# One transformer block on one core: the first feed-forward matrix computed for pairs of segments with seven block products in place of eight

## The chip, the core and the metric

The program runs on one core of a Trainium2 chip. The core has a matrix engine (TensorE, in the profile PE for its matmuls and PEld for its weight loads), a vector engine (VectorE, DVE), an activation engine (ScalarE, ACT), a general engine (GpSimd, POOL) and a queue engine that issues most transfers (SyncE, SP). Each engine works through its own instructions in order; they meet through semaphores. The metric is the device time in microseconds (us). Three timed runs of the kernel before gave 814.06, 815.38 and 816.48 us; their median, 815.38 us, is the time to compare with.

## What is computed

The input x has 2048 rows of 512 numbers, in four segments of 512 rows. A layer norm with a scale and shift taken from a conditioning vector is followed by attention with 32 heads inside each segment, to which a running memory of the earlier segments is added, and by an output projection; then a second layer norm with scale and shift, a feed-forward net with 1792 hidden units, and a gated sum:

```
h = _layernorm(x) * (1 + ca) + sa
x = x + ga * _A_ref(h, A_wq, A_wk, A_wv, A_wo, A_beta)
h = _layernorm(x) * (1 + cb) + sb
x = x + gb * _B_ref(h, B_w1, B_b1, B_w2, B_b2)

def _B_ref(x, w1, b1, w2, b2):
    h = _gelu(x @ w1 + b1)
    return h @ w2 + b2
```

Every value is float32. The kernel keeps each operand of the large products as a high and a low part (suffixes h and l, type fp32r), and computes a product as three: high by high, low by high, high by low.

## The kernel before

Until about 190 us of the profile it makes the projections for queries, keys and values and the memory of all segments. Then comes attention, a loop over 64 positions P (pairs of heads; two of them make one stack Q, four one group U, sixteen a segment). What each engine does in it is written out in a table of tokens and in positions in tenths of P: `ap(pos, f)` puts a piece of work at pos/10. For each P there are score matmuls for the row maximum (four P ahead, line 609, DVE takes the maximum at line 616), score matmuls for the exponentials (line 698, ACT at lines 713 and 724, POOL masks the diagonal at line 701) and the products with V (line 738). A group U then passes through DRAM: `pv_out` stores to TD, `pv_in` loads it as dn and opk, `den` makes the reciprocal and stores RD, `rb_in` loads it spread over rows as rbB, `mix` multiplies and adds (POOL for U below 13, DVE from 13 on), `o_hi` on ACT and `o_lo` make the two parts oh and ol. With the four groups of a segment s done, `wo_part(s, b, g)` (line 815) makes the output projection for each of its four row blocks b, in the bank mm, and `wo_out` (lines 830 to 834) adds x and stores the block to X2D. For segments 0 to 2 this stands in the attention loop, 12 matmuls to a stack; segment 3 follows the loop.

The second layer norm of segment 0 is in the loop too: `ln2_load`, `ln2_stats`, `ln2_rstd`, `ln2_apply`, and `first_ht`, which turns the segment on PE (line 162, 4 instructions for each of 4 blocks of 128 columns), scales it on ACT (line 170, tile C0h) and splits it into C0hh (DVE) and C0hl (POOL, line 141).

The feed-forward part takes one segment after the other, and in it 14 blocks f of 128 hidden units. `ffn1(n)` makes the 12 matmuls of the first matrix into one of three banks f1b (line 989), the gelu on ACT (line 992, tile gt) and the split into gh and gl on DVE; `ffn2(m)` makes the 12 matmuls of the second matrix into the four banks acc (line 1073). The two alternate, with ffn1 four blocks ahead of ffn2. The first four ffn1 and the whole projection of segment 3 stand between the last product with V and the first ffn2. The weights w1 and w2 are loaded, split and kept during the first segment. `xrt` holds x for the last sum, line 1076, from which the output is stored.

## Time and profile before

| | us |
|---|---|
| three timed runs, median (lowest to highest) | 815.38 (814.06 to 816.48) |
| span of the profiled execution, first to last instruction | 811.6 |
| attention loop | about 190 to 484.6 |
| from the last product with V to the first ffn2 | 484.6 to 509.7 |
| ffn1 and ffn2 alternating, to the end | 509.7 to 811 |

The profiled execution is a run of its own; beside its span the page gives no other time for it. The median lies 3.8 us above the span, and that is taken as what lies around it. A row of an engine's timeline has its start and length in us, the engine, the line, what it writes and reads, and in brackets the engine's idle time before it with what ended it. Matmul rows overlap (each is 0.39 us long for 512 columns); the pace is read from start to start. The DMA table says nothing of landing times here; they are read from the rows that waited for a transfer.

### The profile page before, as it was taken

What the parts mean: (1) busy time and instruction counts of PE and PEld (TensorE: products, weight loads), DVE (VectorE), ACT (ScalarE), POOL (GpSimd) and SP (SyncE); (2) the same over time, 40 slices, a digit from 0 to 9 for tenths busy, and PEclk for the clock granted to TensorE, in tenths of its full rate; (3) what the DMA queues carried; (4) which work ended last, traced back from release to release, by engine and by line L of the source; (5) the groups of instructions that cost most, each with busy time, mean ns of one, the idle gap of its engine ahead of it and who ended that gap; (6) DMA issues with size and microseconds to landing.
All of it is one profiled execution on the core that took longest, in us unless ns stands there. A gap on an engine that the chain in (4) does not pass through costs nothing.

```text
span 811.6 us, 13638 instructions
## 1 busy us (share of the span) xinstructions
PE 796.0 (98%) x4669; PEld 546.9 (67%) x4669; DVE 502.7 (62%) x1373; ACT 368.5 (45%) x734; POOL 287.3 (35%) x508
## 2 busy tenths in 40 slices
...
GB/s 339 183 311 253 271 181 218 159 353 129 171 171 182 165 208 175 238 199 181 177 183 206 172 192 192 213 120 101 25 79 1 52 67 38 1 1 104 1 1 52
DMA packets 83566, 123.03 MB, mean 152 GB/s; under 512 B 14116, under 2 KB 46244, under 8 KB 82984
## 3 DMA queue, kind: packets, MB, share of 16 engines
...
q8 instruction: 36, 0.59, 0.3%
...
## 4 chain that ended last, share of the span: by engine, by line
PE 75%; DMA 8%; ACT 5%; DVE 4%; POOL 4%; issue 3%; SPq 1%; ACTq 0%; DVEq 0%; POOLq 0%
PE acc L1073 18%; PE f1b L989 16%; PE pv L738 6%; PE att L698 5%; PE q L330 5%; PE att L609 5%; PE k L330 4%; PE mm L815 3%; PE v L481 3%; DMA RD<-dn 2%; DMA rbB<-RD 2%; ACT pt L713 1%; PE nu L453 1%; DMA qst<-ms 1%; POOL pt L701 1%
## 5 line engine op out<-in xcount | busy, mean ns | idle before, releaser
L616 DVE CUSTOM_DVE_ANT_0 dump<-att,maskb 128x512 bf16<-128x512 f32 (+2 forms) x384 | 192.2, 553 | 27.2 <-PE att L609 24.3
L992 ACT ACTIVATE gt<-f1b,b1t 128x512 f32<-128x512 f32 x56 | 38.5, 688 | 245.8 <-PE f1b L989 195.0
L713 ACT ACTIVATE pt<-att 128x512 f32<-128x512 f32 (+1 forms) x256 | 126.1, 557 | 44.6 <-PE att L698 44.3
L701 POOL TENSOR_SCALAR_AFFINE_SELECT pt<-pt 128x256 f32<-128x256 f32 x256 | 100.1, 408 | 80.1 <-ACT pt L713 50.1
L140 DVE CAST gh<-gt 128x512 fp32r<-128x512 f32 x56 | 23.8, 425 | 163.0 <-ACT gt L992 163.0
L698 PE MATMUL att<-qst,kst 99*128 99x512 bf16 (+3 forms) x512 | 106.6, 300 | 5.5 <-ACT pt L724 2.1
L609 PE MATMUL att<-kst,qst 96*128 96x512 bf16 (+2 forms) x384 | 94.2, 326 | 0.7 <-DVE nm L616 0.2
L738 PE MATMUL pv<-pt,V 128*32 128x512 f32 (+2 forms) x992 | 88.3, 442 | 0.1
L1073 PE MATMUL acc<-w2h,gh 128*128 128x512 f32 (+1 forms) x224 | 86.7, 387 | 0.0
L1073 PE MATMUL acc<-w2l,gh 128*128 128x512 f32 (+1 forms) x224 | 86.0, 384 | 0.4 <-DVE w2l L141 0.4
L1073 PE MATMUL acc<-w2h,gl 128*128 128x512 f32 (+1 forms) x224 | 85.9, 383 | 0.0
L698 PEld LDWEIGHTS <-kst 99*128 99x128 bf16 x512 | 42.9, 97 | 56.9 <-issue 39.7
L989 PE MATMUL f1b<-hodd,w1h 128*128 128x512 f32 x224 | 73.7, 390 | 0.0
L724 ACT ACTIVATE pt<-att 128x512 f32<-128x512 f32 (+1 forms) x128 | 57.1, 512 | 22.9 <-PE att L609 19.9
L153 POOL TENSOR_SCALAR crs<-cmv 128x4 f32<-128x4 f32 x4 | 1.0, 247 | 170.8 <-DVE cmv L150 170.7
L609 PEld LDWEIGHTS <-qst 96*128 96x128 bf16 x384 | 33.2, 98 | 39.9 <-issue 24.6
L1073 PEld LDWEIGHTS acc<-w2l,gh 128*128 128x128 f32 x224 | 42.0, 188 | 9.1 <-DVE w2l L141 0.9
L989 PEld LDWEIGHTS f1b<-hodd,w1h 128*128 128x128 f32 x224 | 42.1, 188 | 8.6
L1073 PEld LDWEIGHTS acc<-w2h,gl 128*128 128x128 f32 x224 | 42.1, 188 | 8.4
L1073 PEld LDWEIGHTS acc<-w2h,gh 128*128 128x128 f32 x224 | 42.1, 188 | 8.3
L738 PEld LDWEIGHTS pv<-pt,V 128*32 128x32 f32 x992 | 22.2, 108 | 36.8 <-issue 26.2
L989 PE MATMUL f1b<-C0hh,w1l 128*128 128x512 f32 x112 | 43.7, 390 | 0.2 <-DVE w1l L141 0.2
...
## 6 DMA issues: line engine op xcount, KB each, us to landing
...
```

Of the source, the lines that this page charges most:

```text
L330: pe.matmul(ps, a[:, k, 128 * g:128 * g + 128], b[k], start=(k == 0 and i == 0), stop=(k == KB - 1 and i == 2))
L481: pe.matmul(ps, a[k][:, 128 * b:128 * b + 128], w[:, k, :], start=(k == 0 and i == 0), stop=(k == KB - 1 and i == 2))
L609: pe.matmul(ps, q_of(P, h, i), k_of(P, h, 128 * (i + 1)), start=True, stop=True)
L616: v.tensor_tensor_reduce(out=dump[n_dump[0] % 2][:, :n], in0=src, in1=maskb[:, 512 - n:], scale=-1.0, scalar=-4 * NEG, op0=ALU.add, op1=AL ...
L698: pe.matmul(ps, k[:99, e, 128 * j:128 * j + 128], q[:99, e, 128 * j:512], start=True, stop=True)
L701: pool.affine_select(out=t, in_=t, pattern=pattern, compare_op=ALU.is_ge, fill=0.0, base=0, channel_multiplier=-1)
L713: act.activation(pt[:, h, :], ps[:, :n], AF.Exp, scale=0.25)
L724: act.activation(pt, pv_, AF.Exp, scale=0.25)
L738: pe.matmul(ps[32 * c:32 * c + 32, lo:hi], V[4 * s + j][:, VW * hd:VW * hd + 32], pt[:, c % 2, lo - o:hi - o], start=start, stop=stop)
L989: pe.matmul(ps, a[:, k, :], b[k], start=(i == 0), stop=(i == 11))
L992: act.activation(g, ps, AF.Gelu_apprx_tanh, bias=b1t[:, f:f + 1])
L1073: pe.matmul((mm if lo else acc[b])[:, lo:hi], a[:, c], w[:, lo:hi], start=(f == 0 and i == 0), stop=(last and i == 2))
```

## The change

The four segments are handled as pairs, 0 with 1 and then 2 with 3: for a pair all of the first matrix, then all of the second. For the first matrix the columns of a pair are one block matrix with two blocks of 256 input features by two segments, and w1 gives for each j from 0 to 6 two blocks of hidden units (f = j and j + 7) by two of input features. `quad(n)` computes that two by two product with seven block products (`prod`, 6 matmuls each: two blocks of 128 features by three parts) where the code before has eight. For this it needs sums and differences of the operands: `r_sub` forms four differences of segment blocks on DVE, once for a pair, `r_hi` and `r_lo` split seven blocks; `w_sub` forms four sums or differences of weight blocks on POOL for each n, `w_hi` and `w_lo` split six of seven views of them in two buffers that alternate (wt1). The products go to the banks bx, by and bv (two each); three of them are added on while the partial sum is copied out by ACT between products (`s1`, `t2`, `s3`), and DVE adds by or bv to the copies (`add`). `g_out` applies the gelu and stores the block to a new DRAM tensor GD; `load_g` brings it back into a ring of four tiles and `split_g` makes gh (ACT) and gl (DVE) for ffn2, two blocks ahead. The work of quad n on t4 and b22 is done within quad n+1, and after the last quad of a pair in a step with no products of its own.

The output projection of segment 2 leaves the attention loop and stands behind it, in the banks bx0, by0, bv0 and spare; the layer norm of segment 1 enters the loop, and its turning (`ln2_turn`, tiles hr) stands between those blocks. The splitting of segment 0 leaves the loop. The weights of the first matrix are loaded and split again for the second pair. ffn2 takes its banks from both sets in turn and the rows for the last sum go through the tile xt2 of segment 2.

```diff
- 'wo': [[2, 10, 10, 10], [6, 10, 11, 11], [2, 10, 10, 11]],
- 'woout': [10, 11, 11],
...
+ 'wo': [[2, 10, 10, 10], [6, 10, 11, 11]],
+ 'woout': [10, 11],
...
- 'ht': 481,
...
- 'ln': [312, 339, 374, 408],
+ 'ht': [465, 474, 481, 494],
+ 'ln': [[312, 339, 374, 408], [560, 597, 612, 624]],
...
- 'w1at': [58, 59, 60],
+ 'w1at': [58, 60],
...
+    def ln2_turn(s, d, ps=None):
+        ps = ps or mm
+        for b in range(4):
+            pe.transpose(ps[:, 128 * b:128 * b + 128], xt2[s][b][:, 128 * d:128 * d + 128], ident)
+        h = ce.tile([128, 512], F32, tag="hr", bufs=8, name=f"hr{s}_{d}")
+        act.activation(h, ps, AF.Identity, bias=cols[:, 2, d:d + 1], scale=cols[:, 3, d:d + 1])
+        hr[s, d] = h
...
+        def load_w1(j):
+            r = wmp.tile([128, 4, 2, 128], F32, tag="wm", bufs=4, name=f"wa{j}")
+            for i in range(2):
+                f = j % FH + FH * i
+                sp.dma_start(r[:, 2 * i:2 * i + 2].rearrange("p a k n -> p (a k) n"),
+                             w1[:, 128 * f:128 * f + 128].rearrange("(k p) n -> p k n", p=128))
+            wa[j] = r
...
-        for s in range(NSEG):
+        for s in range(NSEG - 1):
...
-        def first_ht(d):
-            h, l = transposed(ce, ce, lambda: mm, xt2[0], 0, 2, "C0", 4, 1, (d,),
-                               lo=pool if PRM["htlo"] == "p" else v)
...
-            ap(PRM["ht"] + PRM["htd"] * d, own, "mm", ("h", d), first_ht, (d,), True)
...
+            ap(PRM["ht"][d], own, "mm", ("h", d), ln2_turn, (0, d), True)
...
+        spare = pf.tile([128, 512], F32, name="spare")
+        bx, by, bv = [[pf.tile([128, 512], F32, name=f"{n}{i}") for i in range(2)] for n in ("bx", "by", "bv")]
...
+        def r_sub(p, n):
+            x, y = {"t1": ("b12", "b11"), "t2": ("b22", "b11"), "t3": ("b22", "b12"), "t4": ("b21", "b22")}[n]
+            for o, i, j in zip(hk(p, RAW[n]), hk(p, x), hk(p, y)):
+                v.tensor_tensor(out=o, in0=i, in1=j, op=ALU.subtract)
...
+        def r_hi(p, n):
+            for k in range(2):
+                act.activation(R[n][0][k], hk(p, RAW.get(n, n))[k], AF.Copy)
...
+        def w_sub(j, i):
+            if i == 0:
+                wb[j] = wmp.tile([128, 4, 2, 128], F32, tag="wm", bufs=4, name=f"wb{j}")
+            a, b = wa[j], wb[j]
+            x, y = ((a[:, 2], a[:, 3]), (b[:, 0], a[:, 0]), (a[:, 0], a[:, 2]), (a[:, 1], b[:, 1]))[i]
+            pool.tensor_tensor(out=b[:, i], in0=x, in1=y, op=ALU.add if i == 0 else ALU.subtract)
...
+        def prod(n, name, ps, start):
+            t, i = PW[name]
+            wh, wl = wt1[t][n % 2]
+            rh, rl = R[name]
+            for k in range(2):
+                for c, (a, b) in enumerate(((wh, rh), (wl, rh), (wh, rl))):
+                    pe.matmul(ps, a[:, i, k, :], b[k], start=start and k == 0 and c == 0, stop=k == 1 and c == 2,
+                              skip_group_check=not start)
+        def g_out(n, src, dst, half, seg):
+            f = n % FH + FH * half
+            act.activation(dst, src, AF.Gelu_apprx_tanh, bias=b1t[:, f:f + 1])
+            sp.dma_start(GD[2 * (n // FH) + seg][f], dst)
+        def add(t, ps):
+            v.tensor_tensor(out=t, in0=ps, in1=t, op=ALU.add)
...
+        def quad(n, first, last):
...
+            X, Y, V_, t2 = bx[n % 2], by[n % 2], bv[n % 2], s2[n % 2]
+            X_, V__, t2_ = bx[(n - 1) % 2], bv[(n - 1) % 2], s2[(n - 1) % 2]
+            if not last:
+                prod(n, "b11", X, True)
+                act.activation(s1, X, AF.Copy)
+            if not first:
+                add(s3, V__)
+                g_out(n - 1, s3, s3, 1, 1)
+            step(0)
+            if not last:
+                prod(n, "b21", Y, True)
+                add(s1, Y)
+            step(1)
+            if not first:
+                prod(n - 1, "t4", X_, False)
+            if not last:
+                g_out(n, s1, s1, 0, 0)
+            if not first:
+                g_out(n - 1, X_, s4, 1, 0)
+            step(2)
+            if not last:
+                prod(n, "t2", X, False)
+                act.activation(t2, X, AF.Copy)
+            step(3)
+            if not first:
+                prod(n - 1, "b22", V__, False)
+                add(t2_, V__)
+            step(4)
+            if not last:
+                prod(n, "t1", V_, True)
+            if not first:
+                g_out(n - 1, t2_, t2_, 0, 1)
+            step(5)
+            if not last:
+                prod(n, "t3", X, False)
+                act.activation(s3, X, AF.Copy)
+            step(6)
...
+        for b, ps in enumerate((bx[0], by[0], bv[0], spare)):
+            wops[2, b] = ps
+        for b, ps in enumerate((bx[1], by[1], bv[1], mm)):
+            wops[3, b] = ps
+        rest(15, "pv_in")
...
+        r_hi(0, "b11")
...
+        wo_seg(2, 0, range(4))
+        ln2_turn(1, 0)
...
+        rest(14, "mem_mix", "mix", "o_hi")
+        rest(15, "den", "rb_in")
+        rest(15, "am_in")
...
+        wo_seg(2, 3, range(4))
+        ln2_turn(1, 3)
+        for b in range(4):
+            wo_seg(3, b, range(2))
...
+        for b in range(4):
+            wo_part(3, b, 2)
+        r_lo(0, "t2")
+        rest(15, "mix", "o_hi")
+        r_lo(0, "t1")
+        rest(15, "o_lo")
+        assert not left, left
+        def close_wo():
+            for b in range(4):
...
+        for n in range(2 * FH):
+            j = n % FH
+            if j + 2 < FH:
+                bg(n, 1, load_w1, n + 2)
+                for i in range(4):
+                    bg(n, 5 + i // 2, w_sub, n + 2, i)
+            if j + 1 < FH:
+                for i in range(7):
+                    bg(n, i, w_prep, n + 1, i)
+        bg(0, 1, r_hi, 0, "t3")
+        bg(0, 2, r_lo, 0, "t3")
+        bg(0, 1, ln2_load, 2)
+        bg(0, 3, close_wo)
+        bg(0, 4, r_sub, 0, "t4")
+        bg(0, 5, r_hi, 0, "t4")
+        bg(0, 6, r_lo, 0, "t4")
...
+        for s, n in ((2, 1), (3, 3)):
+            for b in range(4):
+                bg(n, 1 + b, ln2_stats, s, b)
+            bg(n, 5, ln2_rstd, s)
+            for i in range(2):
+                bg(n, 8 + i, ln2_applies, s, 2 * i, 2 * i + 2)
+            for d in range(KB):
+                bg(n, 10 + d, ln2_turn, s, d, (mm, spare)[d % 2])
...
+        ring = [[s1, s2[1 - p], s3, s4] for p in range(2)]
+        def load_g(p, m):
+            sp.dma_start(ring[p][m % 4], GD[2 * p + m // FB][m % FB])
+        def split_g(p, m):
+            h, l = gx[0](f"gh{p}{m}"), gx[0](f"gl{p}{m}")
+            ghs.append((h, l))
+            split(h, l, ring[p][m % 4], v, act)
+        for p in range(2):
+            n = FH * p + FH
+            bg(n - 1, 5, load_g, p, 0)
+            bg(TAIL + n, 5, load_g, p, 1)
+            bg(TAIL + n, 5, load_g, p, 2)
+            bg(TAIL + n, 5, load_g, p, 3)
+            bg(TAIL + n, 6, split_g, p, 0)
+            bg(TAIL + n, 6, split_g, p, 1)
...
+        for i in range(2):
+            fbg(1, i, load_w1, FH + i)
+        for i in range(4):
+            fbg(1, 3, w_sub, FH, i)
+            fbg(1, 12, w_sub, FH + 1, i)
+            fbg(1, 10 + i, w_hi, FH, i)
+            fbg(1, 10 + i, w_lo, FH, i)
...
+        accs = [bx[1], by[1], bv[1], mm], [bx[0], by[0], bv[0], spare]
...
-        for n in range(AHEAD, NSEG * FB + AHEAD):
...
-            if n < NSEG * FB:
-                if n > AHEAD:
-                    ffn1(n)
...
-                ffn2(m)
+        NM = 2 * FB
+        for p in range(2):
+            for j in range(FH + 1):
+                quad(FH * p + j, j == 0, j == FH)
+            xres = xt2[2]
+            for m in range(NM):
+                s, f = 2 * p + m // FB, m % FB
+                if m + 4 < NM:
+                    load_g(p, m + 4)
+                if m + 2 < NM:
+                    split_g(p, m + 2)
...
+                if p == 0 or m < NM - 3:
+                    ffn2(s, f, ghs.pop(0))
         for b in range(4):
-            for m in range(NSEG * FB - AHEAD, NSEG * FB):
-                ffn2(m, (b,))
+            for i, g in enumerate(ghs):
+                ffn2(NSEG - 1, FB - 3 + i, g, (b,))
+        assert not bgs and not fs
```

What the change makes of the engines' orders, at the places that matter for what follows. First PE, at the end of attention; att3 is the bank of the last products with V, pt the exponentials. Before, the first matrix of segment 0 follows at once:

```order
L738 MATMUL att3_2009<-pt63_3_5902,V15_154 32x128 x2
L738 MATMUL att3_2009<-pt62_2_5857,V14_153 32x256 x2
L738 MATMUL att3_2009<-pt63_2_5897,V14_153 32x256 x2
L989 MATMUL f1b0_5946<-C0hh0_0_4974,w1h0_5987 128x512
L989 MATMUL f1b0_5946<-C0hh0_0_4974,w1l0_5988 128x512
L989 MATMUL f1b0_5946<-C0hl0_0_4975,w1h0_5987 128x512
```

With the change the output projection of segment 2 stands there (bx0 from its first group, U = 8):

```order
L737 MATMUL att3_2065<-pt63_3_5898,V15_210 32x128 x2
L737 MATMUL att3_2065<-pt62_2_5851,V14_209 32x256 x2
L737 MATMUL att3_2065<-pt63_2_5893,V14_209 32x256 x2
L814 MATMUL bx0_5943<-woh_2052,oh8_4713 128x512
L814 MATMUL bx0_5943<-woh_2052,ol8_4715 128x512
L814 MATMUL bx0_5943<-wol_2053,oh8_4713 128x512
```

The 48 matmuls of that projection moved from the loop to this place, and the four ffn1 that stood here are gone from it. Next DVE, before the projection of segment 3 is closed. Before (opk15 is the last group's mix, w1l weights, gl a gelu part):

```order
L140 CAST w1h5_5997<-w1r4_5725 128x512
L141 TENSOR_TENSOR w1l5_5998<-w1r4_5725,w1h5_5997 128x512
L787 TENSOR_TENSOR opk15_6007<-opk15_6007,rbB15_6043 128x512
L789 TENSOR_TENSOR opk15_6007<-opk15_6007,amB15_6009 128x512
L804 TENSOR_TENSOR ol15_6128<-opk15_6007,oh15_6126 128x512
L140 CAST gh3_5964<-gt1_5972 128x512
L141 TENSOR_TENSOR gl3_5969<-gt1_5972,gh3_5964 128x512
L1010 TENSOR_TENSOR w2r0_6144<-w2r0_6144,gab_69 128x512 x2
```

With the change (rt1, rt2, rt3 are splits of the segment differences, hr the turned segments, s10 the first partial sum):

```order
L831 TENSOR_TENSOR xb2_3_5657<-spare_5942,xb2_3_5657 128x512
L997 TENSOR_TENSOR rt2l0_5959<-hr1_2_6081,rt2h0_5957 128x512
L997 TENSOR_TENSOR rt2l1_5960<-hr1_3_6105,rt2h1_5958 128x512
L786 TENSOR_TENSOR opk15_5992<-opk15_5992,rbB15_6055 128x512
L788 TENSOR_TENSOR opk15_5992<-opk15_5992,amB15_6057 128x512
L997 TENSOR_TENSOR rt1l0_5963<-hr0_0_4931,rt1h0_5961 128x512
L997 TENSOR_TENSOR rt1l1_5964<-hr0_1_5008,rt1h1_5962 128x512
L803 TENSOR_TENSOR ol15_6183<-opk15_5992,oh15_6179 128x512
L1041 TENSOR_TENSOR s10_5985<-by0_5945,s10_5985 128x512
L1022 TENSOR_TENSOR w1ml1_5980<-wa1_5736,w1mh1_5979 128x512
L997 TENSOR_TENSOR rt3l0_5967<-hr1_0_6022,rt3h0_5965 128x512
L997 TENSOR_TENSOR rt3l1_5968<-hr1_1_6045,rt3h1_5966 128x512
```

The mix of the last group moved behind the splits and differences of the segment blocks, and the first partial sum follows it. Third PE, in the feed-forward part. Before, ffn2 (acc) and ffn1 (f1b) alternate:

```order
L1073 MATMUL acc3_5952<-w2h7_6191,gh1_5962 128x512
L1073 MATMUL acc3_5952<-w2h7_6191,gl1_5967 128x512
L1073 MATMUL acc3_5952<-w2l7_6192,gh1_5962 128x512
L989 MATMUL f1b2_5948<-hodd00_5953,w1h12_5975 128x512
L989 MATMUL f1b2_5948<-hodd00_5953,w1l12_5976 128x512
L989 MATMUL f1b2_5948<-hodd10_5957,w1h12_5975 128x512
```

With the change, at the end of a pair's first matrix (rt4 and rb22 are the last two products' operands, then ffn2 of block 0):

```order
L1032 MATMUL bx0_5943<-rt4l0_5971,w1th0_5981 128x512
L1032 MATMUL bx0_5943<-rt4h1_5970,w1th0_5981 128x512
L1032 MATMUL bx0_5943<-rt4h1_5970,w1tl0_5982 128x512
L1032 MATMUL bx0_5943<-rt4l1_5972,w1th0_5981 128x512
L1032 MATMUL bv0_5947<-rb22h0_5973,w1th0_5981 128x512
L1032 MATMUL bv0_5947<-rb22h0_5973,w1tl0_5982 128x512
L1032 MATMUL bv0_5947<-rb22l0_5975,w1th0_5981 128x512
L1032 MATMUL bv0_5947<-rb22h1_5974,w1th0_5981 128x512
L1032 MATMUL bv0_5947<-rb22h1_5974,w1tl0_5982 128x512
L1032 MATMUL bv0_5947<-rb22l1_5976,w1th0_5981 128x512
L1309 MATMUL bx1_5944<-w2h0_6244,gh00_6847 128x512
L1309 MATMUL bx1_5944<-w2h0_6244,gl00_6848 128x512
```

No product of another block stands between the last products of the first matrix and the first of the second any more. At that place ACT has (s30, s10, s20, s21, s40 are tiles of the ring, a gelu has b1t among its inputs):

```order
L1037 ACTIVATE s21_5987<-s21_5987,b1t_70 128x512
L1091 ACTIVATE s30_5988<-bx0_5943 128x512
L1037 ACTIVATE s30_5988<-s30_5988,b1t_70 128x512
L1037 ACTIVATE s40_5989<-bx0_5943,b1t_70 128x512
L1037 ACTIVATE s20_5986<-s20_5986,b1t_70 128x512
L134 ACTIVATE gh00_6847<-s10_5985 128x512
L134 ACTIVATE gh01_6851<-s21_5987 128x512
L134 ACTIVATE gh02_6856<-s30_5988 128x512
```

and SP has, with GD0 and GD1 the stored blocks of the two segments:

```order
L1038 DMA GD1_5_144<-s21_5987 128x512
L1249 DMA s10_5985<-GD0_0_125 128x512
L1038 DMA GD1_13_152<-s30_5988 128x512
L1038 DMA GD0_13_138<-s40_5989 128x512
L1038 DMA GD1_6_145<-s20_5986 128x512
L1249 DMA s21_5987<-GD0_1_126 128x512
L1249 DMA s30_5988<-GD0_2_127 128x512
L1249 DMA s40_5989<-GD0_3_128 128x512
```

The split of block 0 stands on ACT behind the last gelu of the first matrix, and the loads of blocks 1 to 3 on SP behind the store of that gelu's block.

391 lines of the change are left out of this document (199 added, 192 removed).

## The prediction

> **What bounds the kernel now.** I read the page's first part, then a table of stretches (start and end; of PE, PEld, DVE, ACT and POOL the busy us and count; granted clock, DMA share, GB/s), then the chain of waits in the feed-forward part.
>
> ```profile
> PE 796.0 (98%) x4669; PEld 546.9 (67%) x4669; DVE 502.7 (62%) x1373; ACT 368.5 (45%) x734; POOL 287.3 (35%) x508
> ...
> 460.00:484.60 24.60, 22.75 (x192) 10.88 (x184) 9.45 (x25) 17.13 (x39) 14.53 (x29) 1.00 0.63 176
> 484.60:509.70 25.10, 24.94 (x110) 20.29 (x110) 18.10 (x31) 6.83 (x10) 2.87 (x2) 1.00 0.62 201
> 509.70:811.00 301.30, 298.14 (x1375) 247.70 (x1373) 128.73 (x240) 50.08 (x76) 4.37 (x6) 1.00 0.17 55
> ...
> 526.90 2.72 PE acc L1073 x12
> 529.62 2.72 PE f1b L989 x12
> ```
>
> PE sets the end. From the last product with V (484.6) on it hardly pauses, the clock is 1.00, and DVE, ACT and POOL are at 43%, 17% and 1% after 509.7. Twelve matmuls of 512 columns take 2.72 us whichever matrix they belong to, so one costs 2.72 / 12 = 0.227 us. A matmul less is time gained, if nothing stops PE in its place.
>
> **What is removed.** The first matrix takes 56 blocks of 12 matmuls, 672; with the change 14 quads of 7 products of 6, 588. 84 x 0.227 = **-19.0 us**. The second matrix, the output projection and the 64 transposes stay in number.
>
> **The projection of segment 2 moves out of attention.** Rows of ACT, one per stack (ms is copied once for each):
>
> ```profile
> 411.58 0.27 ACT L132 ACTIVATE ms<-mm 48x128 bf16<-48x128 f32 x1
> 419.55 0.27 ACT L132 ACTIVATE ms<-mm 48x128 bf16<-48x128 f32 x1
> 429.72 0.27 ACT L132 ACTIVATE ms<-mm 48x128 bf16<-48x128 f32 x1
> 438.11 0.27 ACT L132 ACTIVATE ms<-mm 48x128 bf16<-48x128 f32 x1
> 448.53 0.27 ACT L132 ACTIVATE ms<-mm 48x128 bf16<-48x128 f32 x1
> 458.95 0.27 ACT L132 ACTIVATE ms<-mm 48x128 bf16<-48x128 f32 x1
> 468.57 0.26 ACT L132 ACTIVATE ms<-mm 48x128 bf16<-48x128 f32 x1
> ```
>
> A stack without the projection takes 7.97 us (419.55 less 411.58), the three with 12 matmuls of it take 10.42, 10.42 and 9.62: without them 6.5 us less. The last 12 of the 48 stand after 468.57, where the end hangs on something else:
>
> ```profile
> 465.15 3.07 SPq L839 DMA_DIRECT2D w1r<-in_w  x2
> 469.92 0.38 SPq L776 DMA_DIRECT2D RD<-dn  x1
> 478.20 0.69 DVE L787 TENSOR_TENSOR opk<-opk,rbB 128x512 f32<-128x512 f32 x1 [10.66 <-DMA rbB<-RD]
> 479.72 0.63 ACT L132 ACTIVATE oh<-opk 128x512 fp32r<-128x512 f32 x1 [1.70 <-DVE opk L789]
> 482.26 2.35 PE L738 MATMUL att<-pt,V 128*32 128x512 f32 x28 [1.84 <-POOL pt L701]
> ```
>
> RD of group 13 leaves late, since SP is held by a weight load; so rbB, the mix, oh on ACT, the exponentials behind it and the last products with V are late. With the change two w1 loads stand there for three and no store of X2D before RD, so RD can leave up to 2.2 us sooner. I take 1.5 for this piece, between 0 and the 2.7 of its matmuls. One stack, 419.55 to 429.72, is 2.2 us too long without any projection:
>
> ```profile
> 420.38 1.29 POOL L787 TENSOR_TENSOR opk<-opk,rbB 128x512 f32<-128x512 f32 x1 [2.15 <-DMA rbB<-RD]
> 422.96 1.27 POOL L141 TENSOR_TENSOR C0hl<-C0h,C0hh 128x512 fp32r<-128x512 f32 x1
> 426.74 2.18 PE L738 MATMUL pv<-pt,V 128*32 128x512 f32 x8
> ```
>
> POOL waits for rbB and then has the queue of its masks ahead of PE, with C0hl among it. The change takes the four C0hl off POOL: 1.5 us gained (0 to 2.2). But the same wait can come up in stacks 29 to 31, which become as short: 1.0 lost (0 to 2.2). Attention gives 6.5 + 1.5 + 1.5 - 1.0 = 8.5 us, and behind it the 48 matmuls cost 48 x 0.227 = 10.9: **+2.4 us** (0 to +5).
>
> **The stretch behind attention.** Counted from the last product with V, PE has 84 projection matmuls (19.1) and 16 transposes (four take 0.44, quoted below, so 1.8): 20.9 us of cover, then b11 and b21 (2.7). DVE has, up to the mix of group 15, some 21 instructions of 512 columns at 0.69 and some 3 us of others, 17.5 us, and waits inside for ACT, whose weight split waits for POOL's four w_sub and for group 14's products: I make it 22 to 23 us until that mix. Before, the mix began 15.9 us after the last product:
>
> ```profile
> 496.52 0.59 SPq L782 DMA_DIRECT2D rbB<-RD  x1
> 500.55 0.69 DVE L787 TENSOR_TENSOR opk<-opk,rbB 128x512 f32<-128x512 f32 x1 [0.24 <-DMA rbB<-RD]
> 537.79 0.44 PE mm L162 x4
> ```
>
> Mix (two of 0.69), oh (0.63) and the copy of s1, which stands behind oh on ACT, end at about 25.5; PE wants to overwrite that bank with t2 at 23.6 + 0.8, where 0.8 is a wait I expect at the second turning (mm is read by ACT behind the weight split). So 0.8 + 1.15 there and 0.2 at the first t4, whose operand is at the end of DVE's queue: **+2.2 us** (0, if ACT and DVE run ahead, to +7, if the blocking below strikes each DVE instruction beside POOL's).
>
> **From the first to the second matrix, twice.** Behind the last t3 PE's order has t4, b22 and ffn2 without anything between. Rows:
>
> ```profile
> L992 ACT ACTIVATE gt<-f1b,b1t 128x512 f32<-128x512 f32 x56 | 38.5, 688 | 245.8 <-PE f1b L989 195.0 <-issue 43.6 <-DVE opk L789 7.1
> L138 ACT ACTIVATE w2h<-w2r 128x512 fp32r<-128x512 f32 x14 | 8.8, 626 | 3.1 <-DVE w2r L1010 2.9
> L132 ACT ACTIVATE ts<-att 128x512 f32<-128x512 f32 x1 | 0.6, 597 | 1.8 <-PE att L738 1.8
> ...
> L141 DVE TENSOR_TENSOR gl<-gt,gh 128x512 fp32r<-128x512 f32 x56 | 39.7, 710 | 2.0
> L833 DVE TENSOR_TENSOR xb<-acc,xb 128x512 f32<-128x512 f32 x4 | 2.5, 680 | 0.0
> ...
> 509.42 0.39 PE L989 MATMUL f1b<-C0hl,w1h 128*128 128x512 f32 x1
> ...
> 509.91 0.69 ACT L992 ACTIVATE gt<-f1b,b1t 128x512 f32<-128x512 f32 x1 [2.35 <-PE f1b L989]
> ```
>
> From the end of a matmul's slot (509.42 + 0.23) to ACT's start is 0.26. First, t4 adds onto the bank that ACT still copies to s3: 0.26 + 0.60 + 0.04 = 0.9. Second, behind b22 come an addition on DVE, its gelu, the split of block 0 and only then ffn2's second matmul: 0.26 + 0.68 + 0.69 + 0.63 + 0.71 = 2.97, less the first matmul's slot, 2.75. Third, the load of block 1 is queued on SP behind the store of that last gelu. It issues 1.63 + 0.34 after b22 and takes 4.0, as rbB took (496.52 to 500.55); gh and gl add 1.34, so block 1 is whole at 7.3, where PE, after block 0 and its 2.72, would be at 5.5: 1.6 after the slot of a first matmul. Together 5.25, twice **+10.5 us**. Only the third piece is open: with the 5.84 below it is 3.4, and 0 if it lands as fast as RD of group 15, which was issued at 495.04 and let rbB go at 496.52; both entries then take 7.3 to 14.2.
>
> ```profile
> 459.25 5.84 DMA opk<-TD
> ...
> 495.04 0.32 SPq L776 DMA_DIRECT2D RD<-dn  x1
> ```
>
> The Trainium skill ("SBUF — State Buffer", The DMA setup-cost knee) fits a transfer as about 2 us and its bytes at 436 GB/s, an estimate of 2.6 us for 256 KB; the row of rbB says 4.0 here. By the Trainium skill both entries would cost 2.8 us less.
>
> **Covered work.** In a quad of 42 matmuls, 9.5 us, ACT has three copies (1.8), four gelus (2.75) and 1792 columns of weight splits (about 2.2), 6.8 us; DVE three additions and the low parts, 4.5; POOL four w_sub. A partial copy is due 2.7 us after its product and takes 0.9, so 1.8 us are to spare. GD's stores and loads, 256 KB per 2.4 us, are about 110 GB/s where the table of stretches shows 55 now and 176 at the end of attention. Free while this holds; the rival below has the price. The last three blocks wait about 0.3 once for a buffer: **+0.3 us**.
>
> **The sum.** -19.0 + 2.4 + 2.2 + 10.5 + 0.3 = -3.6 us, against a span of 811.6: 808.0. The median of the runs lies 3.8 above the span, so 815.4 - 3.6 = **811.8 us**.
>
> **Rivals.** One: the waits at the seams are covered. Attention returns all 10.9 us (the projection was its only load there), the stretch behind stalls 0, the loads land within 2 us: -19.0 + 0 + 0 + 7.3 + 0.3 = -11.4, 804 us. For it speaks that DVE stood idle 10.66 us at 478.20; against it that the chain through rbB does not shorten with PE's work. Chance 0.2.
>
> Two: DVE is late behind attention. DVE and POOL hinder each other:
>
> ```profile
> 494.90 1.59 POOL L794 TENSOR_TENSOR amB<-amB,rm 128x512 f32<-128x512 f32 x1 [7.47 <-DMA rm<-rdd]
> 495.38 1.67 DVE L141 TENSOR_TENSOR gl<-gt,gh 128x512 fp32r<-128x512 f32 x1
> ```
>
> An instruction of 0.71 took 1.67 while POOL multiplied. POOL has some 7.8 us there (two multiplications of 1.28, eight halves of that); if each delays DVE by a bit over half its length, 4.5 us more: +0.9, 816.3 us. Against it: most falls in DVE's own waits. Chance 0.17.
>
> Three, on the other side: **the quads are bound by the copies.** PE may not add a product to bx before ACT has copied the partial sum, and ACT, in order, may sit at a gelu whose addition waits on DVE. If the four w_sub of a quad (2.6 us) each stop DVE for their whole length, the additions and low parts slip by 2.6, past the 1.8 to spare: 0.8 us in each of 14 quads, 11 us, -3.6 + 11 = +7.6, 823 us. It decides from a delay of 1.8 us per quad on. For it speaks the row of 1.67; against it that DVE idles half of each quad. Chance 0.16. The Trainium skill ("SBUF — State Buffer", SBUF: two separate sides) says that a two-input DVE instruction and a GpSimd one that reads SBUF exclude each other for whole instructions; the row of 1.67 agrees with it, and by that rule this rival is the likelier.
>
> That the change removes fewer products than it says is ruled out by its order: 588 rows of line 1032.
>
> **Numbers.** My forecast has 0.47, the rivals 0.2, 0.17 and 0.16. What a measurement of this kernel can tell from no change is about 0.3%, 2.4 us: faster is below 812.9, slower above 817.8. Of the forecast's 0.47 some 0.32 lie below 812.9 (the third piece and attention decide), 0.10 between, 0.05 above; of rival two 0.03, 0.11, 0.03. Faster 0.32 + 0.2 + 0.03 = 0.55, same 0.21, slower 0.05 + 0.03 + 0.16 = 0.24. The forecast's own range is 806 to 817. For 8 in 10 the range takes in rival one at its middle, rival two and the lower edge of rival three: 804 to 820.
>
> **What would show it.** 84 matmuls fewer, still 2.72 per 12; the last product with V at 476 (475 to 480) in place of 484.6; PE idle between t3 and the first blocks of ffn2 near 5 us at both places, its end set by gl on DVE and by a load on ACT; no PE idle inside quads; at t2 of quad 0 a wait for ACT of about 1 us. Wrong it would be if the quads take more than 9.6 us, or the entries under 3 us, or if attention ends no sooner.

## The result and the profile after

The changed kernel is slower. Its median is 821.43 us (six runs, 818.84 to 826.18) beside 816.45 us for the kernel before on the same chip; the ratio is 1.0076 (95% interval 1.0050 to 1.0102). The forecast was 811.8 us, with 804 to 820 as the range. The profiled execution has a span of 818.8 us, 7.2 more than the one before. By the medians the difference is 5.0 us: this execution took 820.48 us, 1.7 more than its span, so the profiled execution of the kernel before, with the same 1.7, would have taken 813.3, less than each of its timed runs on this chip. The 3.8 us that the prediction put around the span were 1.7 here.

Each time below is given as a ratio to the kernel before, whose runs were taken between those of the experiment on the same chip. The experiments ran on five chips, so kernels of different chips are compared by these ratios alone. A waiting time or a length of the loop is that of one profiled execution.

The first part of the page after, and two rows of PE's timeline one quad apart (start and length in us, engine, line, operation):

```profile
PE 788.6 (96%) x4585; PEld 535.2 (65%) x4585; DVE 555.7 (68%) x1405; ACT 467.8 (57%) x914; POOL 333.9 (41%) x558
...
521.03 0.39 PE L1032 MATMUL by<-rb21h,w1mh 128*128 128x512 f32 x1
...
530.55 0.39 PE L1032 MATMUL by<-rb21h,w1mh 128*128 128x512 f32 x1
```

PE is down from 98% to 96% of a longer span: it has 84 matmuls fewer in the trace as well (4669 to 4585), and waits more. A full quad takes 530.55 - 521.03 = 9.52 us, 42 matmuls at 0.227, so nothing stops PE inside this quad. Most of the time is lost at three places, which this table of stretches shows (columns as in the prediction):

```profile
450.00:460.00 10.00, 7.64 (x40) 2.72 (x36) 4.20 (x15) 4.12 (x10) 2.39 (x7) 0.66 0.64 190
500.00:510.00 10.00, 8.15 (x36) 6.40 (x35) 9.89 (x14) 2.03 (x6) 5.77 (x5) 1.00 0.55 183
510.00:520.00 10.00, 8.86 (x32) 7.22 (x33) 9.05 (x13) 6.48 (x11) 3.60 (x4) 0.83 0.88 296
560.00:580.00 20.00, 20.00 (x94) 16.55 (x93) 12.23 (x19) 14.73 (x26) 2.38 (x3) 1.00 0.54 181
580.00:595.00 15.00, 11.99 (x44) 8.81 (x43) 6.17 (x10) 6.74 (x11) 0.00 (x0) 0.89 0.78 259
```

The first row lies in the last stacks of attention, the next two behind it, the last at the entry to the second matrix; between them, from 560 to 580, PE is busy all of 20 us. The waits themselves, in PE's timeline (qst holds the queries of a stack, which come from QD, and the row maxima, which are copied into it from ms; pt are the exponentials, s the copies of partial sums):

```profile
453.52 1.04 PE L608 MATMUL att<-kst,qst 96*128 96x512 bf16 x2 [2.36 <-DMA qst<-QD]
...
480.76 2.35 PE L737 MATMUL att<-pt,V 128*32 128x512 f32 x28 [0.75 <-POOL pt L700]
...
511.14 0.78 PE L1032 MATMUL bx<-rt2h,w1mh 128*128 128x512 f32 x1 [3.00 <-ACT s L1060]
...
583.04 0.50 PE L1032 MATMUL bx<-rt4h,w1th 128*128 128x512 f32 x1 [0.74 <-ACT s L1091]
...
588.13 0.51 PE L1309 MATMUL bx<-w2h,gh 128*128 128x512 f32 x1 [2.06 <-ACT gh L134]
```

The second row is the last group of products with V: it ends at 480.76 + 2.35 = 483.1, where the kernel before was at 484.6. The loop has given 1.5 us, not 8.5.

A ledger of the two profiled executions. PE's plain work behind the last product with V is the matmuls at 0.227 and the turnings at 0.44 (four instructions each). Before, that is 1392 and 12, 320.8 us of the 327.0 that it took, a loss of 6.2. Only 0.6 of it lies ahead of the first ffn2, where 108 matmuls and no turning stand in 25.1 us: 48 of the projection of segment 3 and 60 of the first matrix, which are five of its blocks and not four. After, it is 1356 and 12, 312.6 us of 335.7, a loss of 23.1. Up to the end of t3 of quad 6, at 582.15, the changed kernel has 378 and 12, 91.0 us, in 99.1, a loss of 8.1: 1.3 up to the end of b21 of quad 0, 3.2 ahead of t2 of quad 0, 1.7 in a slow pace behind it, and 1.9 later, most of it around the turnings of segments 2 and 3. From the end of t3, 36 matmuls (t4, b22 and two blocks, 8.16 us) took 13.7 and 13.3 us at the two entries.

| term | predicted | measured |
|---|---|---|
| 84 matmuls | -19.0 | -19.0 |
| projection of segment 2, behind the loop | +10.9 | +10.9 |
| the loop without it | -8.5 | -1.5 |
| stretch behind the loop | +2.2 | +7.5 (8.1 less 0.6) |
| two entries | +10.5 | +10.7 |
| the rest | +0.3 | -1.3 |
| sum | -3.6 | +7.3 (spans: +7.2) |

### The profile page after: what moved, and what is told of

Same layout as the page of the kernel before. It is cut to its first block, busy times and chain, and to the rows that moved or that the text cites. A ratio compares the mean times of both kernels' runs of the same rounds, so it can differ in the third digit from the quotient of the medians.

```text
span 818.8 us, 14152 instructions
## 1 busy us (share of the span) xinstructions
PE 788.6 (96%) x4585; PEld 535.2 (65%) x4585; DVE 555.7 (68%) x1405; ACT 467.8 (57%) x914; POOL 333.9 (41%) x558
## 4 chain that ended last, share of the span: by engine, by line
PE 75%; DVE 7%; ACT 6%; DMA 6%; issue 3%; POOL 3%; ACTq 0%; SPq 0%; DVEq 0%; POOLq 0%
PE bx L1032 8%; PE pv L737 7%; PE att L697 6%; PE att L608 6%; PE bx L1309 5%; PE q L314 5%; PE by L1309 5%; PE bv L1309 5%; PE bv L1032 4%; PE k L314 4%; PE v L465 3%; PE spare L1309 2%; PE mm L814 2%; PE mm L1309 2%; PE by L1032 2%
## 5 line engine op out<-in xcount | busy, mean ns | idle before, releaser
L700 POOL TENSOR_SCALAR_AFFINE_SELECT pt<-pt 128x256 f32<-128x256 f32 x256 | 101.4, 413 | 82.8 <-ACT pt L712 49.0
L1007 POOL TENSOR_TENSOR wb<-wa 128x256 f32<-128x256 f32 x28 | 26.9, 962 | 155.5 <-DMA wa<-in_w 147.4
L137 DVE TENSOR_TENSOR gl<-s,gh 128x512 fp32r<-128x512 f32 x56 | 39.9, 712 | 69.5 <-ACT gh L134 69.4
L134 ACT ACTIVATE gh<-s 128x512 fp32r<-128x512 f32 x56 | 35.1, 630 | 83.2 <-PE spare L1309 38.9
L1041 DVE TENSOR_TENSOR s<-bv,s 128x512 f32<-128x512 f32 x28 | 19.3, 688 | 37.7 <-PE bv L1032 29.2
L619 DVE TENSOR_REDUCE nm<-att 128x2 f32<-128x256 f32 x64 | 27.2, 426 | 23.5 <-PE att L655 19.2
L1037 ACT ACTIVATE s<-s,b1t 128x512 f32<-128x512 f32 x42 | 30.3, 721 | 16.2 <-DVE s L1041 16.1
L615 DVE DVE_READ_ACCUMULATOR2_ANT nm<- 128x1 f32 x384 | 31.9, 83 | 0.0
L1309 PE MATMUL bx<-w2h,gh 128*128 128x512 f32 (+1 forms) x70 | 26.4, 377 | 4.1 <-ACT gh L134 4.1
L501 POOL TENSOR_SCALAR qp<-qp 128x512 f32<-128x512 f32 x12 | 18.8, 1564 | 23.1 <-ACT qp L496 23.1
L1309 PE MATMUL bx<-w2h,gl 128*128 128x512 f32 (+1 forms) x70 | 26.4, 377 | 0.2 <-DVE gl L137 0.2
L314 PE MATMUL q<-Ahl,wqh 128*128 128x512 f32 x64 | 25.9, 404 | 0.5 <-DVE Ahl L137 0.5
```

Of the source, the lines that this page charges most:

```text
L134: act.activation(hi, src, AF.Copy)
L137: lo_eng.tensor_tensor(out=lo, in0=src, in1=hi.bitcast(F32), op=ALU.subtract)
L314: pe.matmul(ps, a[:, k, 128 * g:128 * g + 128], b[k], start=(k == 0 and i == 0), stop=(k == KB - 1 and i == 2))
L615: v.tensor_tensor_reduce(out=dump[n_dump[0] % 2][:, :n], in0=src, in1=maskb[:, 512 - n:], scale=-1.0, scalar=-4 * NEG, op0=ALU.add, op1=AL ...
L700: pool.affine_select(out=t, in_=t, pattern=pattern, compare_op=ALU.is_ge, fill=0.0, base=0, channel_multiplier=-1)
L1309: pe.matmul(ps, a[:, c], w[:, lo:hi], start=(f == 0 and i == 0), stop=(last and i == 2))
```

## Experiments

**The three stalls taken one at a time.** First the load that enters the loop.

```diff
- 'ln': [[312, 339, 374, 408], [560, 597, 612, 624]],
+ 'ln': [[312, 339, 374, 408], [574, 602, 615, 624]],
```

> Only the 1 MB load of segment 1 (xt from X2D) is issued later, behind the stack's RD, xb and rbB rows on SP in place of right behind the last kst and qst; its statistics follow 5 places later. Theory: this load shares the DMA engines with the last stack's qst, which took 9.12 us from issue to its first reader, and PE's idle 2.36 us then cost a further 2 us at a granted clock of 0.66. Then the interval between ms rows there falls from 13.09 to 8 to 9 us, the granted clock from 450 to 460 is 1.00, and the time falls by 3.5 to 5 us from 821.4, to about 817. Rival: qst is late through its own chain (ms on ACT, the store to QD); then the interval stays near 13 us and the time near 821. In between, if the wait only goes on to RD and rbB of group 13: the interval falls, the next one grows from 9.50 by as much, and the time stays within 1 us.

Ratio 1.0075 (1.0046 to 1.0104): no gain. The interval of 13.09 fell to 7.72, but its neighbours show where the wait went:

```profile
447.74 0.77 PE L697 MATMUL att<-qst,kst 99*128 99x512 bf16 x3 [1.51 <-DMA qst<-ms]
464.54 0.77 PE L697 MATMUL att<-qst,kst 99*128 99x512 bf16 x3 [1.66 <-DMA qst<-ms]
474.20 1.04 PE L697 MATMUL att<-qst,kst 99*128 99x512 bf16 x2 [3.48 <-DMA qst<-ms]
```

It is no longer qst that is late but the 12 KB of row maxima that go from ms into it, and they are late in three stacks. From the tenth last ms row (the texts ahead of the runs call it that of stack 24) to the end of the last product with V it is 102.0 us; this is called the loop's length below, and it is 102.4 before and 100.4 after. So the load is not the cause by itself.

Then the clock, with matmuls in the gaps at the entries.

```diff
+            if last:
+                fill(n, 3)      # ahead of t4
...
+            if last:
+                fill(n, 9)      # behind b22
```

> Twelve matmuls whose result nothing reads are added at each entry to the second matrix: 3 ahead of t4 of the last quad, 9 behind b22, into a bank that is free. They are 0.7 and 2.0 us of work where PE idles 0.74 and 2.06 us. Theory: the idle time lets the granted clock fall for one stretch of 3.4 us behind each entry (8 matmuls at 0.43 us in place of 0.227), so with PE busy the stretch runs at 0.227 and each entry costs 1.6 us less: 821.4 - 3.2 = 818.2, and the granted clock of 589 to 593 and 736 to 740 is 1.00. Rival: the slow matmuls there wait on operands, not on the clock; then nothing is gained, and the time is 821 to 822.

Ratio 1.0057 (1.0028 to 1.0086): no gain that can be told from the change alone. The granted clock is 1.00 at both entries, but they still lose 4.55 and 4.69 us, the added matmuls counted as lost, against 5.53 and 5.15 in the change. In e1_load_late one entry had no slow stretch without any added matmul, and lost 4.56. So the clock is about 1 us of an entry, and the rest is waiting for data.

Then the order of the entry.

```diff
+                bg(n - 1, m, load_raw, p, m)        # m = 0, 1
+                bg(n - 1, 5 + m, split_g, p, m)
+            bg(n - 1, 6, load_g, p, 2)
+            bg(TAIL + n, 0, ahead, p, 0)            # ffn2 of block 0, ahead of t4
+            bg(TAIL + n, 0, load_g, p, 3)
+            bg(TAIL + n, 4, split_g, p, 2)
+            bg(TAIL + n, 4, ahead, p, 1)            # ffn2 of block 1, behind b22
```

> Blocks 0 and 1 of the second matrix, whose operands were written to GD six quads earlier, are loaded in the quad before the last and split there, and their 24 matmuls stand ahead of t4 and behind b22 of the last quad; blocks 2 and 3 load into the two tiles that the stretch has free first. Theory: an entry costs its 5.3 us because PE's order has only work there that hangs on the last copies and gelus. With 5.44 us of other work between, the copy of s3 (0.9), the addition, gelu and split (2.75) and the next load are all covered: PE idle at both entries falls from 2.8 us each to under 0.5, the clock stays 1.00, and the time falls by 9 to 10.6, to 811 to 812.5. Rival: the loads and splits put into the last full quad collide there with the weights of the second matrix on ACT and DVE and its loads on SP; then the quad grows by 2 us or more and the gain is 5 us or less, 816 or more.

Ratio 0.9965 (0.9938 to 0.9991), 8 to 9 us under the change and a little faster than before. The same stretches of this kernel:

```profile
580.00:590.00 10.00, 10.00 (x45) 8.07 (x44) 4.86 (x8) 5.80 (x10) 0.00 (x0) 1.00 0.84 285
590.00:600.00 10.00, 10.00 (x45) 8.26 (x44) 7.26 (x12) 5.70 (x10) 0.00 (x0) 1.00 0.83 292
```

PE does not pause; the loss at the two entries is 0.18 and 0.14 us. The 10.7 us were a matter of order, with the two tiles more that the new order needs, and the first matrix's gain shows once they are gone.

Last the POOL instructions behind the loop.

```diff
-        for i in range(4):
-            w_sub(1, i)          # behind wo_x(3, 3)
...
+        for j in range(2):       # behind pv_in of group 15
+            for i in range(4):
+                w_sub(j, i)
```

> The four w_sub of quad 1 are taken from behind the last amB on POOL to right behind the four of quad 0, into POOL's idle time from 489 to 502. Theory: behind attention DVE is late because POOL's two-input instructions hold it up: beside w_sub and amB from 502.2 to 508, four r_sub took 3.59 us for 2.5, two w_lo 0.96 each for 0.41, and two r_lo 1.82 for 1.29, 2.7 us in all, and the mix of group 15 hangs on it, then oh and the copy of s1 on ACT, then t2 on PE (3.00 us idle, and 1.6 us more at a low granted clock). With POOL free there the mix comes 2 us or more sooner, t2's wait falls under 1 us, and the time falls by 3 to 4.5, to 817 to 818.5. Rival: DVE's own queue and ACT decide; the instructions that POOL now meets earlier are lengthened in its place, DVE had no slack there, and the time stays within 1 us of 821.4.

Ratio 1.0043 (1.0016 to 1.0070), by the ratios 2.7 us under the change where 3 to 4.5 were expected. The two intervals overlap, so the time alone does not show the gain; the rows do show the mechanism. DVE's rows after, beside POOL's of the same microseconds:

```profile
500.84 3.59 DVE L989 TENSOR_TENSOR hr<-hr,hr 128x512 f32<-128x512 f32 x4
504.36 0.96 DVE L1022 TENSOR_TENSOR w1tl<-wa,w1th 128x256 fp32r<-128x256 f32 x1
...
503.85 1.18 POOL L1007 TENSOR_TENSOR wb<-wa 128x256 f32<-128x256 f32 x1
```

and in this kernel, where POOL is idle there, with two rows from later on:

```profile
500.80 2.49 DVE L989 TENSOR_TENSOR hr<-hr,hr 128x512 f32<-128x512 f32 x4
503.21 0.42 DVE L1022 TENSOR_TENSOR w1tl<-wa,w1th 128x256 fp32r<-128x256 f32 x1
...
523.53 0.60 ACT L1060 ACTIVATE s<-bx 128x512 f32<-128x512 f32 x1 [5.57 <-DMA GD<-s]
524.18 0.69 PE L1032 MATMUL bx<-rt2h,w1mh 128*128 128x512 f32 x1 [3.65 <-ACT s L1060]
```

The rows are short again, the mix of group 15 comes 22.5 us after the last product with V instead of 25.4, and t2 of quad 0 waits 1.23 us instead of 3.00. Then a new wait shows, 3.65 us in quad 1: the copy of s1 stands until the store of s1 to GD has left. I put that to the 1 MB load of segment 2, ahead of the store in SP's queue; the next kernel has it in pieces, among other edits, so this cause was not tested by itself.

**The stalls together.**

```diff
+            if n == 0:
+                rest(15, "o_hi")                    # now behind the copy of s1
+                r_lo(0, "t1")
+                rest(15, "o_lo")
...
-        bg(0, 1, ln2_load, 2)
+        for b, (n, i) in enumerate(((0, 4), (0, 6), (1, 1), (1, 3))):
+            bg(n, i, ln2_piece, 2, b)
```

> The entry order of e3_entry and the early w_sub of e4_wsub_early together, with two more edits: in quad 0 ACT copies s1 before oh of group 15 instead of behind it, and the loads of segments 2 and 3 (1 MB each from X2D) go out as eight pieces of 256 KB over quads 0 to 2, with the statistics of segment 2 one quad later. Theory: what is left of the stall behind attention is ACT's order (in e4_wsub_early the copy of s1 stood 0.5 us behind oh, which waited for the mix; t2 waited 1.23 us) and a store of s1 late behind the 1 MB load (the copy of s1 of quad 1 waited 4.88 us for it and t2 of quad 1 3.65 us). Then both waits go under 1 us and the time is 4 to 6 us under the 813.3 of e3_entry: 807 to 809. Rival: DVE's queue is what is late; then close_wo, which needs oh and ol of group 15, waits in place of t2, 1.5 to 2.5 us, and the time is 810.5 to 812.

Ratio 0.9953 (0.9932 to 0.9974), 1 us under e3_entry by these ratios, which the intervals do not tell apart, so closer to the rival. Both waits at t2 are gone; in their place stand 1.21 us for hr in the turnings, 1.00 for rt4l and 0.92 for a block that DVE normalises.

**The step on the loop.** The projection of segment 2 goes back where it was.

```diff
- 'wo': [[2, 10, 10, 10], [6, 10, 11, 11]],
+ 'wo': [[2, 10, 10, 10], [6, 10, 11, 11], [2, 10, 10, 11]],
...
-        wo_seg(2, 0, range(4))
-        ln2_turn(1, 0)
+        ln2_turn(1, 0, bx[0])
```

> One part of the change is undone: the projection of segment 2 stands in the attention loop again, in the places that it had before, and the four turnings of segment 1 behind the loop use four banks. By the prediction's step the loop gave 6.5 to 8.5 us for taking it out, so with it the length from the ms row of stack 24 to the last product with V goes from 100.5 to 103.8 (the four profiles with this loop so far) to 107 to 112. Theory now: the three stacks are set by chains through DMA (qst, and ms into qst), and the projection ran in their waits; then the length stays at 101 to 104.5. Behind the loop PE has 10.9 us less work, but the mix of group 15 still comes 23 to 26 us after the last product with V, so that part is turned into idle time ahead of t2: I expect 2 to 6 us less in all by the theory, 816 to 820, and by the prediction's step no gain or a loss, 821 to 825.

Ratio 1.0049 (1.0024 to 1.0075). ACT's ms rows of the last stacks, this kernel:

```profile
440.05 0.27 ACT L128 ACTIVATE ms<-mm 48x128 bf16<-48x128 f32 x1
450.47 0.27 ACT L128 ACTIVATE ms<-mm 48x128 bf16<-48x128 f32 x1
460.89 0.27 ACT L128 ACTIVATE ms<-mm 48x128 bf16<-48x128 f32 x1
470.52 0.26 ACT L128 ACTIVATE ms<-mm 48x128 bf16<-48x128 f32 x1
```

and the change:

```profile
438.75 0.27 ACT L128 ACTIVATE ms<-mm 48x128 bf16<-48x128 f32 x1
446.68 0.27 ACT L128 ACTIVATE ms<-mm 48x128 bf16<-48x128 f32 x1
459.77 0.27 ACT L128 ACTIVATE ms<-mm 48x128 bf16<-48x128 f32 x1 [0.47 <-PE mm L676]
469.27 0.27 ACT L128 ACTIVATE ms<-mm 48x128 bf16<-48x128 f32 x1 [0.83 <-PE mm L676]
```

With 36 matmuls more in them three stacks take 470.52 - 440.05 = 30.5 us, and PE is busy in all of them; without them they take 30.5 as well in the change, with waits. In the next four profiles of the changed loop they take 28.3 to 30.2, but there the last piece, from the last ms row to the last product with V, is longer (14.5 to 17.0 us, beside 13.8 in the change and 14.3 here). The loop's length is 101.0 with the projection (101.4 to 104.0 in the four later kernels that have it) and 99.9 to 103.8 in five profiles without it. This is where the prediction's step fell: the projection in the loop was free, within this spread. Behind the loop PE's 10.9 us less turned into waits of 4.20 and 5.21 us (for oh of group 14 and for the copy of s1), and a slow pace behind them:

```profile
496.73 0.54 PE L814 MATMUL bx<-woh,oh 128*128 128x512 f32 x1 [4.20 <-ACT oh L128]
...
509.55 0.80 PE L1032 MATMUL bx<-rt2h,w1mh 128*128 128x512 f32 x1 [5.21 <-ACT s L1060]
```

**Why the stacks do not shorten.** The load in four pieces, earlier:

```diff
+                if i:
+                    ap(ln[0] + 1 + 14 * b, ln2_piece, i, b)     # ln[0] = 505
```

> Only the load of segment 1 is changed: four pieces of 256 KB in stacks 25 to 27 instead of 1 MB behind the last kst and qst. Theory: with nothing large on the DMA engines in the last three stacks, qst and ms into qst come in time, and those three intervals between ms rows, 28.5 to 30.5 us in all in the four profiles with the 1 MB load, fall to 24.5 to 26.5; the attention length falls to 96.5 to 99.5 and the time by 3 to 4, to 817 to 818.5. Rival: the three stacks are set by the row maxima's own chain (DVE, POOL, PE, ACT, a small transfer) and by POOL's masks whatever else is moved; then the three stay at 28 us or more and the time within 1 us of 821.4. If the pieces only move the waits to stacks 25 to 27, the length stays and those intervals grow by 2 us or more.

Ratio 1.0065 (1.0042 to 1.0088). The three intervals are 8.18, 13.45 and 8.05, in all 29.7: qst is again 3.14 us late, now without the large load.

```profile
456.13 1.03 PE L612 MATMUL att<-kst,qst 96*128 96x512 bf16 x2 [3.14 <-DMA qst<-QD]
```

Next, the other loads leave the last stacks:

```diff
- 'w1at': [58, 60],
+ 'w1at': [64, 65],
...
+        for b in range(4):
+            wo_x(2, b)            # behind the loop
```

> As e7_load_pieces, with the pieces closer together (all ahead of the last kst and qst), and the other loads that need not be in the last stacks put behind the loop: the four xb of segment 2 and both wa. So the last three stacks carry only their own kst, qst, TD, opk, amB, rm and rbB. Theory: those stacks are bound by the DMA engines (share 0.78 to 1.03 from 440 to 452, qst 9.1 to 9.6 us from issue to its reader where a stack lasts 8), and the projection filled the wait; then the three intervals fall from 28.5 to 30.5 to 24 to 25.5, with no wait for qst over 0.5 us, and the attention length is 95 to 98. Rival: the chain of the row maxima and POOL's masks set them; then the waits for nm and pt stay (1.6 and 0.8 to 2.4 us) and the three stay at 27 us or more. Behind the loop w_sub, and with it w1mh, waits for wa some 4 us more and the additions wait for xb, so the time itself is no test: 818 to 826 either way.

Ratio 1.0107 (1.0042 to 1.0173; two runs), not a test of time. The last two intervals are 7.70 and 8.05, but the pieces, closer together, moved the waits to the stacks ahead (11.34, 8.01, 11.96; 2.54 us for ms into qst), and the length is 99.5. Undecided. So these loads and two more were taken out of the last stacks, the load of segment 1 as a whole and rm. Without rm the kernel no longer computes the block; one execution was made, of 836.33 us, and only its loop is read:

```diff
-                rm = so.tile([128, 512], F32, tag="rbB", bufs=2, name=f"rm{U}")
...
-                opks[U, "rm"] = rm
+                opks[U, "rm"] = am
...
+        for b in range(4):
+            ln2_piece(1, b)       # with its statistics, behind the loop
```

> As e8_quiet, and in addition the load of segment 1 with its statistics stands behind the loop, and rm is not loaded for groups 12 to 15 (POOL multiplies amB by itself there, so the product is another one, and its time the same). The last four stacks move only kst, qst, TD, opk, amB, RD and rbB, 1.3 MB each against about 1.9. Theory (transfers): no wait for qst from QD or from ms over 0.5 us from stack 28 on, four intervals between ms rows of 7.7 to 8.3, 31 to 33 in all (38.5, 38.5, 36.8 and 36.5 in the profiles with all loads), and the attention length 94 to 97. Rival (the maxima's chain and POOL): waits of 1.5 to 2.5 us for ms into qst or for nm stay, and the four are 35 or more. Behind the loop the time grows by 10 us or more in either case, so only the loop is read.

```profile
438.66 0.27 ACT L128 ACTIVATE ms<-mm 48x128 bf16<-48x128 f32 x1
446.67 0.27 ACT L128 ACTIVATE ms<-mm 48x128 bf16<-48x128 f32 x1
455.04 0.27 ACT L128 ACTIVATE ms<-mm 48x128 bf16<-48x128 f32 x1
462.75 0.27 ACT L128 ACTIVATE ms<-mm 48x128 bf16<-48x128 f32 x1
471.40 0.27 ACT L128 ACTIVATE ms<-mm 48x128 bf16<-48x128 f32 x1 [0.83 <-PE mm L680]
```

Four intervals in 471.40 - 438.66 = 32.7 us, and no wait for qst; the one wait over 0.5 us in those stacks is for nm, 1.59. The loop's length is 94.2, that is 8.2 us under the kernel before and 6.3 under the change. Two rows of the stretches, the change first, then this kernel, show the DMA engines (last but one column):

```profile
448.00:452.00 4.00, 3.16 (x38) 1.44 (x30) 3.04 (x13) 3.79 (x9) 2.25 (x6) 1.00 1.03 280
```

```profile
448.00:452.00 4.00, 3.99 (x41) 1.74 (x34) 3.51 (x14) 3.66 (x9) 3.92 (x7) 1.00 0.62 162
```

A DMA share of 1.03 where PE then waits, 0.62 where it does not. This run also takes the statistics and normalisations of segment 1 off DVE in the last stacks, and in the change three of the statistics (0.66 to 0.69 us each) stand on DVE just ahead of the reciprocal that RD stores; so a part of what is gained may be theirs. The waits for qst and for ms into qst are transfers. Which single transfer decides was not isolated.

**A version that beats both.** The edits of e5_tail_entry with the projection back in the loop, and another order behind it:

```diff
+        rest(15, "den", "rb_in", "am_in")           # ahead of w_lo(0, 1)
...
+        for b in range(4):
+            bg(0, 1, wo_part, 3, b, 2)              # between b21 and t2 of quad 0
```

> All edits of e5_tail_entry, the projection of segment 2 in the attention loop again as in e6_wo2_back, and behind the loop another order on DVE, ACT and POOL: both sets of w_sub ahead of amB of group 14, the denominators of group 15 and r_sub t1 ahead of the split of the second weight part, the third quarter of the projection of segment 3 between b21 and t2 of quad 0. Theory: the loop takes the projection for nothing (length 101 to 104), and behind it the 14 to 16 us of DVE work, no longer in wait for POOL and ACT, let t2 start 15 to 17 us after the last product with V, where PE has 15.4 us of work; so most of the 10.9 us comes out: 5 to 9 us under e5_tail_entry, 803.5 to 807.5. Rival: the chain TD, RD, rbB of group 15, three transfers of 3 to 4 us each in a row, holds back the last quarter of the projection and with it the banks of quad 1; then t2 or close_wo waits 4 us or more and the time is 809 to 812.

Ratio 0.9936 (0.9907 to 0.9965), not told apart from e5_tail_entry by these intervals. In the profiled execution (814.28 us, the longest of five with a median of 808.78) PE waited 2.34 and 0.64 us for oh and ol of group 14 and 1.30 for oh of group 15, and 21 matmuls ran at 0.427 us behind it. Two ways to get these back were tried, 20 matmuls that nothing reads, and an order that spares DVE:

```diff
+        bg(0, 1, fill, 13)
...
+            fill(7)                                  # ahead of the last quarter
```

> Only matmuls whose result nothing reads are added to e9_wo2_order, into a free bank: 13 ahead of the third quarter of the projection of segment 3 and 7 ahead of the last quarter, where PE stood idle for 2.34 + 0.64 and 1.30 + 0.23 us. Theory: there the idle time has a second price, the granted clock, since behind it nothing but PE sets the pace: 13 + 8 matmuls went at 0.427 us in place of 0.227, 4.2 us. With PE kept busy the granted clock of 500 to 520 is 1.00 and the time falls by 3 to 4.5 from 808.8, to 804.3 to 805.8. Rival: as in e2_fill, what comes behind waits for its data in any case; then the clock is 1.00 and the time stays within 1 us of 808.8, or grows by the 20 matmuls where the data were there sooner (up to 2 us).

Ratio 0.9956 (0.9940 to 0.9972). The granted clock of the whole execution is 0.998, and the time no better: 0.64, 1.22 and 1.02 us of waits stand behind the added matmuls, for ol, the copy of s1 and oh. The rival held, as far as the intervals tell: what sets this stretch is DVE and ACT, not PE's pace.

```diff
+            w_sub(1, i, v)                           # on DVE, behind r_lo t1
...
-        bg(0, 3, close_wo)
+        bg(0, 5, close_wo)
```

> No added matmuls; only the order behind the loop is changed against e9_wo2_order: the four w_sub of quad 1 run on DVE, late, in place of POOL beside rb11l, w1ml and rb21l; the mix of group 14 goes ahead of r_sub t3 and t2, so that its oh and ol, and the loads for group 15 behind it on SP, come sooner; and the last quarter of the projection stands behind t1 of quad 0 in place of behind t2. Theory: a w_sub of 0.73 us on POOL keeps DVE from starting, or doubles the row it meets (2.39 and 2.30 us for 1.29), where on DVE it takes 0.41. The rows of rb11l, w1ml and rb21l go back to 1.29, 0.69 and 1.29, 2.6 us; mix 14 begins 3 us sooner; PE's waits of 2.34, 0.64 and 1.30 fall to under 1.5 in all, and most of the slow clock with them: 5 to 7 us less, 802 to 804. Rival: the mix of group 14 is set by rbB (issued 491.34, some 4 us), not by DVE, and with a wait for it ahead of r_sub t3 and t2, t2 comes no sooner; then the waits only change places and the time stays at 807 to 810.

Ratio 0.9996 (0.9972 to 1.0020), the worst of the three. The first half of the theory held: rb11l, w1ml and rb21l take 1.29, 0.68 and 1.29 us with POOL out of the way. The second half did not: the copy of s1 now stands on ACT behind the later weight split (t2 waits 3.15 us), and quad 1 waits 2.65 us for the additions of the later projection. Two edits at once, so which of them cost most is open.

```diff
-                bg(n, 10 + d, ln2_turn, s, d, (mm, spare)[d % 2])
+                bg(n, 13 + d, ln2_turn, s, d, (mm, spare)[d % 2])
```

> As e9_wo2_order, with the turnings of segments 2 and 3 three places later in their quads, since PE waited 0.92 and 0.56 us there for the last block that DVE normalises, and matmuls behind it ran 0.2 us longer each for 8 to 13 of them. Expected: those waits go to 0 and the time falls by 1 to 2.5 from 808.8, to 806.5 to 808. Rival: the later turnings meet the gelus on ACT, which reads the turned bank, and PE waits for hr instead; then the time is the same within 1 us.

Ratio 0.9890 (0.9853 to 0.9928), median 805.40 us (803.27 to 809.55) beside 814.54: faster than both kernels. The interval meets that of e9_wo2_order, so what the later turnings gain is not told apart from nothing. The two waits in the turnings are gone as expected; 2.77 and 1.69 us for oh of groups 14 and 15 remain behind the loop, and t4 of quad 0 waits 0.87 for the copy of s3.

## Why the prediction was wrong

- **The 84 matmuls and their pace** were right: 42 in 9.52 us.
- **The loop is the step that failed:** "the three with 12 matmuls of it take 10.42, 10.42 and 9.62: without them 6.5 us less". In the two profiles these three stacks took 30.5 us with the projection and 30.5 without it. The 7.97 that stood for a stack without it was taken from one with less to transfer (149 GB/s in it, 204 to 231 in the last three after). Taken out, the projection did not shorten the last stacks: it left their waits for qst and for ms into qst bare, which it had filled (e6_wo2_back). With the transfers of other work gone as well, the loop is 8.2 us shorter (e13_no_loads), so PE's part of the step was about what I said, but another resource stood behind it. That this resource is the transfers is shown by the waits and by this one run, in which the statistics went too; a run with the projection back and these transfers gone was not made. I read PE as the bound because it was busy, and did not ask how late qst could come; its landing stood in no row, since nothing waited for it. The argument stood in the prediction, against the first rival ("the chain through rbB does not shorten with PE's work"), and was not turned on my own term.
- **The other pieces of the loop.** C0hl off POOL was right: the interval of 10.17 us became 8.29 in the profile after (8.6 to 9.8 in the next four), up to 1.9 for the 1.5 predicted. So was the piece behind the last ms row, 16.0 before and 13.8 after, 2.2 for 1.5. But the three intervals ahead of C0hl's are some 0.8 us longer each in every profile with the changed loop, 2.5 us that the prediction did not have. The turnings of segment 0 stand earlier, one, two and one in these intervals for none, one and one before, and I had moved them at no cost. The third interval has as many as before, so they do not explain all of it, and no run took them out: the cause is open.
- **The stretch behind the loop** was right in kind and too small, 7.5 for 2.2. At t2 of quad 0, where 1.15 was given, the copy of s1 behind oh of group 15 made PE wait 3.00 us, and 1.7 more went in the slow pace behind the wait, which had no term. The wait is larger because the mix of group 15 came at 25.4 us for the 22 to 23 counted, and this is the second rival: POOL's w_sub and amB lengthen DVE's rows, and without w_sub there the mix comes at 22.5 (e4_wsub_early). Another 1.9 us, around the turnings of segments 2 and 3 in the quads, had no term either. The Trainium skill ("SBUF — State Buffer", SBUF: two separate sides) has the two engines exclude each other for whole instructions; rows of 0.96 beside POOL and 0.42 without agree.
- **The entries** were right in size, 10.7 for 10.5, and partly by luck in the pieces: the copy of s3 (0.74) and the chain to gh (2.06) were as told, no wait for the load of block 1 came, and a slow clock took its place. Where the clock stayed full, at the first entry of e1_load_late, the second matmul of block 1 did wait, about 0.5 us for its gl, where the prediction had 1.6; the slow clock cost about 1 us on top of that.
- **The third rival,** quads bound by the copies, gave the nearest figure and the wrong reason: PE is busy 20.00 of 20 us from 560 to 580, within the quads.
